# Blocks 11 and 12: q and k turned by DMA instead of by TensorE, and one x turned a unit sooner

## Chip, core and metric

One core of a Trainium2 chip runs the whole kernel. The metric is device time in microseconds; the time before is the median of three runs, 305.38 us (305.3 to 307.37). The profile comes from one further execution.

## What is computed

Attention in a sliding window with distance penalties, and behind it a layer norm and a two-layer MLP with a residual:

```python
scores = (q @ k.T) / sqrt(64) + slope[h] * -|i - j|     # only 0 <= i - j < 128
x = softmax(scores) @ v                                 # 8 batches, 8 heads, 576 tokens, 64 a head
x = x.transpose(0, 2, 1, 3).reshape(8, 576, 512)
xn = (x - mean) / sqrt(var + 1e-6) * g_ln
out = x + relu(xn @ w_ch1) @ w_ch2                      # 512 -> 2048 -> 512
```

Inputs and output are float32; the kernel loads them as float16 by casting DMAs and accumulates in float32.

## The kernel before

**Blocks and pairs.** The batches are taken two at a time (p = 0 to 3). The 576 tokens of such a pair of batches make nine blocks of 128 rows: blk 0 to 7 alternate between the two batches, and blk 8 holds the 64-token tails of both. Numbered through, there are 36 blocks; block n is (p, blk) = divmod(n, 9). q and k are loaded in pairs of blocks: (p, i) is the pair of blk 2i and 2i+1, so pair (1, 1) is blocks 11 and 12, (1, 2) is 13 and 14, (1, 3) is 15 and 16. The members of a pair are called its first and second half below.

**Turning q and k.** The scores need q and k with the 64 head elements on the partitions. There are two ways. With `turn` the pair is loaded in four DMAs (L256), TensorE makes 64 small transposes (L350, 32 for q and 32 for k) into two PSUM banks of the pool `ps_mm`, which has four, and VectorE and ScalarE copy one q and one k each out of them (L369, L370). With `turn_natural` the pair is loaded in six DMAs of another layout (q in four, L280; k in two, L277), and SyncE issues one transposing DMA for each half of q and of k (L383). The function `by_dma` decides: a pair goes by DMA if its number is at least `TURN_BY_DMA`, which is 13.

**The groups.** After attention, the blocks go through the MLP in groups: GROUPS = four of 2 blocks (groups 0 to 3), then seven of 4. A group has 16 units of the first layer (`mlp1`, L876 for the matmuls and L892 for the ScalarE relu, each unit filling one `ps_mm` bank) and a second layer (`mlp2`, L906), whose output a VectorE instruction (L1252) finishes and SyncE stores (L1272). The first layers of groups 0 and 1 run interleaved, as `mlp1_pair`.

**The order of the work** is written out by hand. TensorE, VectorE, ScalarE, SyncE and GpSimd run their instructions in the order of the program. `steps` is a list of attention steps; `weave_at(units, *places)` lays step after step behind the numbered units of a group, a place for each step. Before the loop stand the steps of blocks 0 to 9; from n = 8 the loop makes for each n four steps: values of block n (`values_at_once`, L598, with its x, L607), the turn of pair n + 3 where that is by TensorE, `centre` (xc, L639, with a transposing DMA of xc into xT on SyncE, L649), the scores of block n + 2 (`attend`, L502, exp on ScalarE, L513), the masks (L535) and the square of xc (L683). For pairs that go by DMA, q is issued with block m = n + 5 and k with m = n + 6 (`turn_natural` in `third`). Blocks 0 to 7, 10 and 11 have their x turned by TensorE (`turn_x`, L659); in groups 0 and 1 a VectorE or ScalarE instruction copies it out with the gain g (L666, L671).

**The queues.** GpSimd issues all loads in one order, AHEAD = 7 blocks ahead of the values; each of its DMAs waits on the one eight before it. Raw q and k tiles come from a pool of four for each tag (`raw_pool`); a load into a reused tile waits for the readers of that tile, TensorE's transposes or the transposing DMAs. SyncE issues the stores and the transposing DMAs of q, k and xc, in program order, each waiting on the SyncE DMA eight before. The turned tiles are pools of four (q) and five (k).

In the two lines of the loop that matter here, and in the place list of the interleaved first layers (L1308), the code before reads:

```python
if n + 3 < count and order[n + 3][1] % 2 == 0 and not by_dma(*order[n + 3]):
    step += turn_step(n + 3)          # n = 8: blocks 11 and 12
...
weave_at(mlp1_pair((0, 12), (0, 8), (12, NFB), (8, NFB)), 1, 2, 3, 3, 7, 7, 10, 18, 24, 28)
```

The seventh place, 10, belongs to the step x_step(3), the turn of block 3's x (L659 on TensorE, L666 on VectorE); unit 12 of that list is group 1's first, which reads it.

Of the kernel before, what the change touches and what calls it, by code (L numbers as in the profile page):

```python
# [39 lines left out]

SEVEN = 4

TURN_BY_DMA = 13

# [51 lines left out]
def kernel(  # L98
# [15 lines left out]
    NFB = FFN // P  # L114
# [5 lines left out]
    def pool(name, bufs, **kw):  # L120
        return ctx.enter_context(tc.tile_pool(name=name, bufs=bufs, **kw))
# [163 lines left out]
    def by_dma(p, blk):  # L285
        return p * NSLOT + blk >= TURN_BY_DMA

# [9 lines left out]
    order = [(p, blk) for p in range(NPAIR) for blk in range(NSLOT)]  # L297
# [393 lines left out]
    def inv_std(first, n):  # L691

        blocks = slice(first, first + n)
        rs = rstd[:, blocks]
        aa = small.tile([P, 4], FP32, tag="aa", name="aa")[:, 0:n]
        hh = small.tile([P, 4], FP32, tag="hh", name="hh")[:, 0:n]
        nc.vector.tensor_scalar(
            out=aa, in0=moments[:, blocks, 1], scalar1=EPS, scalar2=None, op0=ALU.add
        )
        nc.vector.tensor_scalar(  # L700
            out=hh.bitcast(I32),
            in0=aa.bitcast(I32),
            scalar1=1,
            scalar2=None,
            op0=ALU.logical_shift_right,
        )
        nc.vector.tensor_tensor(
            out=rs.bitcast(I32), in0=magic[:, 0:n], in1=hh.bitcast(I32), op=ALU.subtract
        )
        for _ in range(2):  # L710
            nc.vector.tensor_tensor(out=hh, in0=rs, in1=rs, op=ALU.mult)
            nc.vector.scalar_tensor_tensor(
                out=hh, in0=hh, scalar=-0.5, in1=aa, op0=ALU.mult, op1=ALU.mult
            )
            nc.vector.scalar_tensor_tensor(
                out=rs, in0=hh, scalar=1.5, in1=rs, op0=ALU.add, op1=ALU.mult
            )
# [11 lines left out]
    def turn_step(n, *how):  # L729
        p, blk = order[n]  # L730
        return [(turn, p, blk // 2) + how]

    def scores_step(n):
        return [(scores,) + order[n]]

    def values_steps(n):
        p, blk = order[n]
        ahead = place[min(n + AHEAD, count - 1)]
        return [
            [(load_until, ahead), (masks, p, blk), (values, p, blk, 0)],  # L740
            [(values, p, blk, 1), (centre, p, blk)],
        ]

    def x_step(n, copy=nc.vector.tensor_copy):
        return [(turn_x,) + home[n] + order[n] + (copy,)] if n < BY_DMA or n in IN_HASTE else []

    def variance_of(n):

        return [(variance, n)] + [(inv_std, n - 3, 4)] * (n % 4 == 3)

    def masks_of(n, *halves):
        return [(masks,) + order[n] + halves]

    def warm_step(n):
        return [[(warm, n)]]
# [3 lines left out]
    steps = warm_step(5) + [[(slopes,), (decay, m_full)]]  # L759
# [22 lines left out]
    steps += [[(decay, m_tail)] + x_step(5) + masks_of(6), scores_step(7) + variance_of(4), values_steps(6)[0]]  # L782

    steps += [values_steps(6)[1], x_step(6) + masks_of(7), *values_steps(7)]
    first_by_dma = order[TURN_BY_DMA][0], order[TURN_BY_DMA][1] // 2
    steps += [x_step(7) + variance_of(5) + variance_of(6) + [(turn_natural, "k") + first_by_dma]]
    steps += [turn_step(8) + variance_of(7), scores_step(8) + turn_step(9)]
    steps += [[(scores_tail, 0)] + scores_step(9) + masks_of(8) + masks_of(9)]


    for n in range(8, ONE_GO):
# [14 lines left out]
        for tag, m in (("q", n + 5), ("k", n + 6)):  # L806
            if m < count and order[m][1] % 2 == 0 and by_dma(*order[m]):
                p, blk = order[m]
# [9 lines left out]
    for n in range(ONE_GO, count):  # L818
# [12 lines left out]
        for tag, m in (("q", n + 5), ("k", n + 6)):  # L831
            if m < count and order[m][1] % 2 == 0:
                p, blk = order[m]
# [10 lines left out]
    def advance_to(n):  # L844
        nonlocal done
        while done < min(n, len(steps)):
            for f, *args in steps[done]:
                f(*args)
            done += 1
# [4 lines left out]
    def mlp1_pair(*spans):  # L854

        both = mlp1(0, (0, 1)), mlp1(1)
        last = [0, 0]
        for n, (first, end) in enumerate(spans):
            assert last[n % 2] == first
            last[n % 2] = end  # L860
            for _ in range(first, end):
                yield next(both[n % 2])
        for units in both:
            assert next(units, None) is None

    def mlp1(g, on_dve=()):
        xT = turned_x[g]
        w = w1 if g < FIRST_GROUPS else w1g
        cols = len(members[g]) * P

        at = g % 2 * cols if len(members[g]) == 2 else 0
        ht = hidden[g] = ht_all[:, :, at : at + cols]
        for fb in range(NFB):
            ps = ps_mm.tile([P, 4 * P], FP32, tag="mm", name="ps_m1")
            for kb in range(NKB):
                nc.tensor.matmul(  # L876
                    ps[:, 0:cols],
                    w[:, kb, fb * P : (fb + 1) * P],
                    xT[:, kb, 0:cols],
                    start=(kb == 0),  # L880
                    stop=(kb == NKB - 1),
                )
            if fb in on_dve:
                nc.vector.tensor_scalar(
                    out=ht[:, fb, :],
                    in0=ps[:, 0:cols],
                    scalar1=0.0,
                    scalar2=None,
                    op0=ALU.max,
                )  # L890
            else:
                nc.scalar.activation(  # L892
                    out=ht[:, fb, :], in_=ps[:, 0:cols], func=AF.Relu
                )
            yield cols
# [32 lines left out]
    def sum_w2(i):  # L928

        c = slice(4 * (i // 4), 4 * (i // 4) + 4)  # L930
        out, a, b = [(t1, b12, b11), (t3, b22, b12), (t2, b22, t1), (t4, b21, t2)][i % 4]
        minus(out[:, c], a[:, c], b[:, c])
# [343 lines left out]
    def weave_at(units, *places, seven=None, sums=None, more={}):  # L1276


        advance_to(done + places.count(-1))
        for u, _ in enumerate(units):  # L1280
            for f, *args in more.get(u, []):
                f(*args)
            if seven is not None:
                if u == 1:
                    inv_std(sum(GROUPS[:seven]), len(members[seven]))
                for i, c in SUMS_AT.get(u, []):
                    sum_hidden(seven, i, c)
            if sums is not None and u % 4 == 1:
                sum_w2(sums + u // 4)
            advance_to(done + places.count(u))  # L1290


    def start():
        nc.sync.dma_start(out=first_tables, in_=tables_dram[:, 0 : 3 * P])
        nc.sync.dma_start(out=g_sb, in_=moe_g_ln.rearrange("(kb p) -> p kb", p=P))
        load_until(place[7])
# [7 lines left out]
    with tc.manual_schedule(engines={engine.PE}):  # L1304
        with tc.manual_schedule(engines={engine.Activation, engine.DVE, engine.SP, engine.Pool}):
            start()
            advance_to(first)
            weave_at(mlp1_pair((0, 12), (0, 8), (12, NFB), (8, NFB)), 1, 2, 3, 3, 7, 7, 10, 18, 24, 28)  # L1308
            weave_at(mlp2(0, ((0, 8), (8, 12), (12, NFB))), 1, 4, 8, 10, 10, 12)
            weave_at(mlp2(1), 1, 3, 5, 7, 9, 13, 13)  # L1310
            weave_at(mlp1(2), 0, 4, 7, 9, 14)
            weave_at(mlp2(2), 1, 5, 9, 13, 13, 15, 15)

            weave_at(mlp1(3, (9, 10, 11)), 4, 7, 8, 10, 12, 15, sums=0)
            weave_at(mlp2(3), 0, 2, 3, 6, 9, 11, 12, sums=4)
            last = len(GROUPS) - 1
            for g in range(4, last):
                one, two = LEAD[g - 4]  # L1320
                early, late = ({u: [(sum_w1, i)] for u, i in at.items()} for at in W1_SUMS_AT.get(g, ({}, {})))
                if g == last - 1:
                    late[20] = [(sum_x, last, i) for i in (1, 2)]
                    late[24] = [(sum_x, last, i) for i in (3, 4)]
                    late[26] = [(inv_std, sum(GROUPS[:last]), len(members[last]))]
                late[4] = [(sum_hidden, g, 4, (0, half))]
                weave_at(mlp1(g, (6, 13)), *one, seven=g, more=early)
                weave_at(mlp2_seven(g), *two, more=late)
            units = mlp2_last(last)
            scores_psum.close()  # L1330
            ps_last = pool("ps_last", 1, space=PSUM)
            LAST_SUMS_AT = {
                u: [(sum_hidden, last, 3 + u % 2, (c, c + half // 2))]
                for u, c in ((2, 0), (4, half // 2), (3, 0), (5, half // 2))
            }
            mlp1_last(last, lambda: next(units), ps_last)
            weave_at(units, more=LAST_SUMS_AT)
# [31 lines left out]
```

## Time and profile before

| | |
|---|---|
| median of 3 runs | 305.38 us |
| the profiled execution | 304.42 us, of which its span 302.6 us |
| TensorE busy | 292.3 us (97%) |
| VectorE, ScalarE, GpSimd busy | 233.0, 184.9, 113.7 us |
| granted TensorE clock, mean | 0.998 |
| DMA, mean over the span | 126 GB/s |

Between the span and the time of the profiled execution lie 1.8 us. PE's busy time counts pipelined matmuls, so that a busy PE may still be slowed; the chain of waits tells which engine ends last at each point. SPq rows are what SyncE issues, POOL's DMA rows what GpSimd issues; a transfer's landing is given from its issue on.

### The profile page before, as it was taken

What the parts mean: (1) busy time and instruction counts of PE and PEld (TensorE: products, weight loads), DVE (VectorE), ACT (ScalarE), POOL (GpSimd) and SP (SyncE); (2) the same over time, 40 slices, a digit from 0 to 9 for tenths busy, and PEclk for the clock granted to TensorE, in tenths of its full rate; (3) what the DMA queues carried; (4) which work ended last, traced back from release to release, by engine and by line L of the source; (5) the groups of instructions that cost most, each with busy time, mean ns of one, the idle gap of its engine ahead of it and who ended that gap; (6) DMA issues with size and microseconds to landing.
All of it is one profiled execution on the core that took longest, in us unless ns stands there. A gap on an engine that the chain in (4) does not pass through costs nothing.

```text
span 302.6 us, 9271 instructions
## 1 busy us (share of the span) xinstructions
PE 292.3 (97%) x3783; PEld 201.0 (66%) x3783; DVE 233.0 (77%) x617; ACT 184.9 (61%) x338; POOL 113.7 (38%) x153
## 2 busy tenths in 40 slices
PE   7788999999999999999999999999999999999994
PEld 2367755866855578646865686568656865788883
DVE  3587778789996788668866886687798878878982
ACT  6577777868967883478357735674577456506500
POOL 8933768883773471594107170760000000000000
PEclk9999999999999999999999999999999999999999
DMA  9999999999999999999999999999571143006014
GB/s 93 167 197 204 192 170 165 196 149 102 143 132 177 164 157 116 156 206 140 95 156 136 128 104 172 168 132 101 122 126 27 38 101 74 20 17 141 3 35 104
DMA packets 150234, 38.03 MB, mean 126 GB/s; under 512 B 140688, under 2 KB 146080, under 8 KB 150192
## 3 DMA queue, kind: packets, MB, share of 16 engines
q0 software_dynamic: 103792, 18.46, 86.6%
q1 hardware_dynamic: 45840, 18.60, 38.7%
q8 instruction: 29, 0.48, 0.7%
q10 hardware_dynamic: 560, 0.39, 0.5%
q14 instruction: 13, 0.11, 0.1%
HBM read 36.90 MB, written 9.44 MB: 153 GB/s over the span
## 4 chain that ended last, share of the span: by engine, by line
PE 87%; DMA 4%; POOL 3%; DVE 2%; ACT 1%; issue 1%; DVEq 0%; POOLq 0%
PE ps_m L876 35%; PE ps_s L1106 22%; PE ps_m L906 9%; PE ps_sc L502 5%; PE ps_sc L598 4%; PE ps_q L1184 4%; DMA w<-in_moe_w_ch_dram 4%; PE ps_x L1000 3%; POOL vx L291 1%; POOL first L192 1%; DVE probs L535 1%; PE ps_pv L569 1%; PE ps_tr L350 1%; PE ps_t L1000 1%; PE ps_s L1000 1%
## 5 line engine op out<-in xcount | busy, mean ns | idle before, releaser
L876 PE MATMUL ps_m<-xT,w1g 128*128 128x512 f16 (+1 forms) x512 | 104.0, 353 | 0.1
L892 ACT ACTIVATE ht_all<-ps_m 128x512 f16<-128x512 f32 (+1 forms) x143 | 72.0, 511 | 38.3 <-PE ps_m L876 36.4
L876 PEld LDWEIGHTS <-w1g 128*128 128x128 f16 x512 | 47.7, 98 | 41.4 <-issue 0.3
L513 ACT ACTIVATE probs<-ps_sc 128x1024 f16<-128x1024 f32 x56 | 56.1, 1022 | 9.6 <-PE ps_sc L502 9.6
L291 POOL DMA_DIRECT2D vx<-in_v_dram x40 | 35.4, 893 | 67.8 <-PE ps_sc L598 59.7
L1106 PE MATMUL ps_s<-w,s 128*128 128x256 f16 x384 | 45.7, 273 | 0.0
L1106 PEld LDWEIGHTS <-s 128*128 128x128 f16 x384 | 36.8, 98 | 4.3 <-issue 0.2
L535 DVE TENSOR_TENSOR probs<-probs,m 128x1024 f16<-128x1024 f16 x56 | 36.3, 685 | 1.6 <-ACT probs L513 1.6
L1106 PE MATMUL ps_s<-w,ht_all 128*128 128x256 f16 x288 | 36.1, 273 | 0.0
L683 ACT ACTIVATE junk<-xc 128x512 f16<-128x512 f16 x28 | 17.7, 631 | 26.9 <-DVE xc L639 26.9
L906 PE MATMUL ps_m<-w,ht_all 128*128 128x512 f16 x128 | 31.5, 380 | 0.0
L1106 PEld LDWEIGHTS <-ht_all 128*128 128x128 f16 x288 | 27.4, 98 | 4.9
L926 DVE TENSOR_TENSOR s<-ht_all 128x1024 f16<-128x1024 f16 (+2 forms) x36 | 20.5, 571 | 11.9 <-ACT ht_all L892 10.9
L280 POOL DMA_DIRECT2D q<-in_q_dram x40 | 27.6, 707 | 4.2 <-PE ps_m L876 1.8
L502 PEld LDWEIGHTS <-k 64*64 64x64 f16 x1088 | 15.5, 107 | 13.5 <-issue 11.6
L607 DVE SCALAR_TENSOR_TENSOR x<-ps_sc,rec 128x512 f16<-128x512 f32 x32 | 22.1, 692 | 1.1
L1127 DVE SCALAR_TENSOR_TENSOR o<-ps_s,rstd,x 128x256 f32<-128x256 f32 x48 | 20.9, 478 | 2.6 <-PE ps_s L1106 2.2
L502 PE MATMUL ps_sc<-q,k 64*64 64x128 f16 (+1 forms) x1088 | 21.1, 211 | 1.2 <-ACT k L424 0.6
L277 POOL DMA_DIRECT2D k<-in_k_dram x20 | 17.9, 912 | 5.7 <-DMA k<-k 5.3
L606 DVE RECIPROCAL rec<-ps_sc 128x8 f32<-128x8 f32 x32 | 6.5, 204 | 16.3 <-PE ps_sc L598 16.2
L598 PEld LDWEIGHTS <-probs 128*128 128x128 f16 x384 | 15.9, 98 | 3.6
L906 PEld LDWEIGHTS <-ht_all 128*128 128x128 f16 x128 | 11.0, 98 | 10.6
(116 smaller groups left out, 374.6 us busy)
## 6 DMA issues: line engine op xcount, KB each, us to landing
out_dram<-o SPq DMA_DIRECT2D x64, 128.0 KB, 3.5
vx<-in_v_dram POOLq DMA_DIRECT2D x32, 128.0 KB, 6.8
w<-in_moe_w_ch_dram POOLq DMA_DIRECT2D x8, 512.0 KB, 11.3
k<-in_k_dram POOLq DMA_DIRECT2D x30, 128.0 KB, 7.2
q<-in_q_dram POOLq DMA_DIRECT2D x48, 64.0 KB, 5.6
q<-in_q_dram POOLq DMA_DIRECT2D x10, 128.0 KB, 5.3
out_dram<-o SPq DMA_DIRECT2D x9, 64.0 KB, 1.9
k<-in_k_dram POOLq DMA_DIRECT2D x8, 64.0 KB, 7.1
```

The costliest lines, as they stand in the source:

```text
L280: nc.gpsimd.dma_start(out=t[half, b], in_=tokens.rearrange("h (c r) d -> r c h d", r=2)[r],)
L291: nc.gpsimd.dma_start(out=vx[p0 : p0 + n, :, 0:D], in_=v[b, :, t0 : t0 + n, :].rearrange("h p d -> p h d"),)
L502: nc.tensor.matmul(in_halves(ps[cols, j, n, t, :])[:, r, queries], kt[rows, hp, cols], in_halves(qt[rows, b, hp])[:, r, queries], start=no ...
L513: nc.scalar.activation(out=dst.rearrange("p (n j) q -> p j n q", j=2), in_=ps.rearrange("p j n t q -> p j n (t q)"), func=AF.Exp, scale=in ...
L535: nc.vector.tensor_tensor(out=dst, in0=dst, in1=mask, op=ALU.mult)
L598: nc.tensor.matmul(ps[:, h, 0 : D + 1], pr[:, h, t, :], vext[(p * NSLOT + o) % NV][:, h, :], start=(n == 0), stop=(n == len(terms) - 1),)
L607: nc.vector.scalar_tensor_tensor(out=x.rearrange("p (h d) -> p h d", h=H), in0=ps[:, :, 0:D], scalar=1.0, in1=rec.unsqueeze(2).broadcast_t ...
L876: nc.tensor.matmul(ps[:, 0:cols], w[:, kb, fb * P : (fb + 1) * P], xT[:, kb, 0:cols], start=(kb == 0), stop=(kb == NKB - 1),)
L892: nc.scalar.activation(out=ht[:, fb, :], in_=ps[:, 0:cols], func=AF.Relu)
L906: nc.tensor.matmul(sums[at], ht[:, fb, at * P : (at + 1) * P], w2[:, fb, :], start=(fb == 0), stop=(fb == NFB - 1),)
L1106: nc.tensor.matmul(ps[:, pair, :], lhs[:, fb, at : at + P], rhs[:, fb, :], start=(first and pair == 0 and fb == 0), stop=(fb == half - 1), ...
L1127: nc.vector.scalar_tensor_tensor(out=outs[at][:, cols], in0=ps[:, pair], scalar=rstd[:, n : n + 1], in1=(xs[p, blk] if fresh else outs[at] ...
```

## The change

`TURN_BY_DMA` goes from 13 to 11, so that pair (1, 1), blocks 11 and 12, is loaded in the natural layout and turned by four transposing DMAs. They are issued, k before q, in the step that before issued the k of pair (1, 2): the step of x_step(7), behind unit 14 of the third group's first layer (`mlp1(2)`). The k of pair (1, 2) is issued at the end of the last step before the loop, that of the tail scores, of the scores of block 9 and of the masks of blocks 8 and 9. In the loop, the turn of pair (1, 1) by TensorE at n = 8 goes away. The place of x_step(3) goes from 10 to 9.

```diff
-TURN_BY_DMA = 13
+TURN_BY_DMA = 11
...
-    first_by_dma = order[TURN_BY_DMA][0], order[TURN_BY_DMA][1] // 2
-    steps += [x_step(7) + variance_of(5) + variance_of(6) + [(turn_natural, "k") + first_by_dma]]
+    (p, first_pair) = order[TURN_BY_DMA][0], order[TURN_BY_DMA][1] // 2
+    by_dma_first = [(turn_natural, tag, p, first_pair) for tag in "kq"]
+    steps += [x_step(7) + variance_of(5) + variance_of(6) + by_dma_first]
     steps += [turn_step(8) + variance_of(7), scores_step(8) + turn_step(9)]
     steps += [[(scores_tail, 0)] + scores_step(9) + masks_of(8) + masks_of(9)]
+    steps[-1].append((turn_natural, "k", p, first_pair + 1))
...
-            weave_at(mlp1_pair((0, 12), (0, 8), (12, NFB), (8, NFB)), 1, 2, 3, 3, 7, 7, 10, 18, 24, 28)
+            weave_at(mlp1_pair((0, 12), (0, 8), (12, NFB), (8, NFB)), 1, 2, 3, 3, 7, 7, 9, 18, 24, 28)
```

In the instruction streams, SyncE's order becomes: k of (1, 1) twice, q of (1, 1) twice, two stores, k of (1, 2) twice, the xc of block 8, two stores, q of (1, 2) twice. Before, the k of (1, 2) stood ahead of the first two stores, and nothing of (1, 1) was there. On GpSimd, the loads of pair (1, 1) are six in place of four, and the first load of q of pair (1, 3) waits for the two transposing DMAs of q of (1, 1) to be done, since it takes their raw tile; before, it waited for TensorE, and the k of (1, 3) waited for the transposing DMAs of k of (1, 2).

## The prediction

> **What bounds the kernel now.** I read the page first, then the chain of waits, then the timelines of SyncE's and GpSimd's queues round the place of the change.
>
> ```profile
> span 302.6 us, 9271 instructions
> ...
> PE 87%; DMA 4%; POOL 3%; DVE 2%; ACT 1%; issue 1%; DVEq 0%; POOLq 0%
> ```
>
> The chain runs through TensorE for 87% of the span, so an edit pays what it takes off TensorE's own stream, or off one of the few stretches where another engine ends last. The change touches two such stretches. The first is in the timeline near 25 us:
>
> ```profile
> 23.34 1.48 PE L876 MATMUL ps_m<-xT,w 128*128 128x256 f16 x12 [0.80 <-DMA w<-in_moe_w_ch_dram]
> 23.52 0.35 DVE L639 TENSOR_SCALAR xc<-x,mean 128x512 f16<-128x512 f16 x1
> ...
> 25.09 0.69 DVE L666 TENSOR_TENSOR xT<-ps_tx,g_sb 128x512 f16<-128x512 f16 x1 [1.22 <-PE ps_tx L659]
> ...
> 25.84 1.92 PE L876 MATMUL ps_m<-xT,w 128*128 128x256 f16 x16 [0.35 <-DVE xT L666]
> ```
>
> TensorE does three units, transposes block 3's x, does one more unit and then stands 0.35 us until VectorE has written xT. The second stretch is in the chain of waits (start, length, what), and, behind it, one TensorE row of the timeline. L513 is the exp of block 10's scores, L683 the square of block 8's xc, L892 the first relu:
>
> ```profile
> 71.75 0.73 PE ps_tr L350 x64
> ...
> 72.51 0.58 ACT q L369
> 73.09 0.64 ACT k L370
> 73.73 0.89 ACT own L513
> 74.62 0.61 ACT junk L683 x2
> 75.22 0.28 ACT ht_all L892
> ...
> 76.40 0.29 PE ps_sc L502 x8
> ...
> 78.41 2.30 PE ps_m L876 x20
> ...
> 85.03 0.49 PE ps_sc L598 x16
> 85.52 0.32 PE ps_sc L502 x8
> ...
> 97.25 0.52 PE ps_sc L502 x31
> ```
>
> ```profile
> 73.43 2.71 PE L876 MATMUL ps_m<-xT,w1g 128*128 128x256 f16 x20
> ```
>
> The 64 transposes of pair (1, 1) are on the chain with 0.73 us. Behind them the chain leaves TensorE: ScalarE's two copies push its exp, its square and then the first relu, and TensorE's fifth unit waits for a PSUM bank. The twenty matmuls from 73.43 take 2.71 us; the same twenty from 78.41, where nothing holds them, take 2.30. So 0.41 us are a stall that the turn causes. The rows at 76.40, 85.52 and 97.25 are the scores of blocks 11, 13 and 15: by then the turned q and k of their pairs must have landed.
>
> **The x a unit sooner.** The same matmuls run in another order: two units, the transposes, two units. Block 3's xc ends at 23.87; the second unit ends at about 23.34 + 8/12 of 1.48 = 24.33, so the transposes wait for nothing, VectorE starts half a microsecond sooner, and its 0.69 us end before the fourth unit does. The stall of 0.35 goes: bounds 0 (the weights of a later chunk hold TensorE instead; behind 25.84 no wait on a DMA stands in the chain before 72 us) and 0.35. I take 0.35.
>
> **The turn taken off TensorE.** Removed: 0.73 us of transposes, four copies, two PSUM banks. Between 0.73 (the stall stays) and 0.73 + 0.41 = 1.14 come off. Does the stall go? The first unit would start 0.73 sooner, at 72.70, and the fifth four units of 2.30/5 later, at 74.54. It needs the first relu. VectorE's side:
>
> ```profile
> 72.04 0.69 DVE L607 SCALAR_TENSOR_TENSOR x<-ps_sc,rec 128x512 f16<-128x512 f32 x1
> ...
> 73.78 0.36 DVE L639 TENSOR_SCALAR xc<-x,mean 128x512 f16<-128x512 f16 x1
> 74.06 0.74 DVE L1252 SCALAR_TENSOR_TENSOR o<-ps_m,rstd,x 128x512 f32<-128x512 f32 x1
> ```
>
> Between x (ends 72.73) and xc stand only the copies and a small mean, so xc8 ends near 73.3 in place of 74.14; ScalarE's exp is done by then, its square adds 0.61 and the relu 0.28: 74.2. That is in time by 0.3 us. I take 1.1. The full gain is then 0.35 + 1.1 = 1.45 us.
>
> [...]
>
> **What is added to the queues.** SyncE and GpSimd:
>
> ```profile
> 66.11 3.10 SPq L383 DMA_TRANSPOSE k<-k  x2
> 69.31 1.18 SPq L1272 DMA_DIRECT2D out_dram<-o  x2
> 74.30 1.20 SPq L649 DMA_TRANSPOSE xT<-xc  x1
> 75.59 1.20 SPq L1272 DMA_DIRECT2D out_dram<-o  x2
> 76.96 4.21 SPq L383 DMA_TRANSPOSE q<-q  x2
> ...
> 82.66 2.50 SPq L383 DMA_TRANSPOSE k<-k  x2
> 85.32 3.05 SPq L383 DMA_TRANSPOSE q<-q  x2
> ```
>
> ```profile
> 51.80 1.42 POOL L256 DMA_DIRECT2D q<-in_q_dram  x2
> 53.15 1.43 POOL L256 DMA_DIRECT2D k<-in_k_dram  x2
> ...
> 60.34 1.83 POOL L277 DMA_DIRECT2D k<-in_k_dram  x2 [0.20 <-PE ps_m L876]
> ...
> 65.16 2.74 POOL L280 DMA_DIRECT2D q<-in_q_dram  x4
> 73.16 1.77 POOL L277 DMA_DIRECT2D k<-in_k_dram  x2 [5.26 <-DMA k<-k]
> ```
>
> And the time from issue to landing (from the view of a tile, for a short window), in this order: k of (1, 1) loaded at 53.15; the two transposing DMAs from 66.11; that of q's first half at 76.96; that at 85.32.
>
> ```profile
> DMA to landing us min/median/max: 6.7/6.9/7.2
> DMA to landing us min/median/max: 5.1/5.4/5.6
> DMA to landing us min/median/max: 8.5/8.5/8.5
> DMA to landing us min/median/max: 8.8/8.8/8.8
> ```
>
> *Loads of (1, 1).* q takes 2.74 instead of 1.42, k 1.83 instead of 1.43: 1.7 us more on GpSimd. k goes from 54.5 to 56.4 and, 6.9 later, has landed by 61.4 and 62.4. The two loads more cover themselves: GpSimd waits later anyhow, 5.26 us ahead of 73.16.
>
> *k and q of (1, 1) on SyncE.* SyncE is free long before 66.11 (it stood waiting for the k of (1, 2)). k goes at 61.5, 2.5 to 3.1 us for two; q behind it, to 66.5 to 70.7 by its own issue times of 3.05 and 4.21. q's first half, issued at 64.0 to 64.6, lands 5.4 to 8.8 later, at 69.4 to 73.4. Block 11's scores come at 76.40 - 1.45 = 74.95. Cover of 1.5 us at least; the price with the cover gone is one for one.
>
> *The wait on GpSimd.* The loads of (1, 3) now start when q's second half of (1, 1) is done: issued about 66, landed at 71 to 75. Behind them are queued v, the tails' q and k, and all later loads. k of (1, 3) then starts 2.74 later, at 74 to 78 instead of 73.16, and its first half lands some 6.9 on, at 81 to 85. SyncE reaches that k only at 82.66, so at most 2.3 us show there. q of (1, 3) behind it landed at 85.32 + 8.8 = 94.1; block 15's scores run at 97.25, so with 0.85 us gained just 2.3 us of delay are covered.
>
> *q of (1, 2) is what is late next.* Before, its first half landed at 76.96 + 8.5 = 85.46, and block 13's scores run at 85.52: nothing to spare. With the gain, TensorE is there at 84.07. On SyncE, ahead of that q: the stores end at 70.1 (0.35 sooner), k of (1, 2) takes 2.5 to 3.1, to 72.7 to 73.3; the xc of block 8 is ready near 73.0 and takes 1.20, the stores 1.20, and with 0.1 between each, q starts at 75.6 to 76.0. Landing at 8.5: 84.1 to 84.5, late by 0 to 0.4. Its time to land is the open price. From below, 5.4; the nearest row is its own, 8.5; but it now has the k of (1, 2) close ahead in the queue, and beside it the loads of q of (1, 3), which before were issued at 65.16. These now fall into a lull, of which this is a row of the busy time by stretch (the last two numbers are the DMA share and GB/s):
>
> ```profile
> 72.00:74.00 2.00, 2.00 (x74) 1.38 (x63) 1.93 (x7) 1.49 (x3) 0.84 (x1) 1.00 0.19 62
> ```
>
> The lull takes part of what is added, so I put 0.4 on the 8.5: late by 0.4 to 0.8, middle 0.6. From above, 8.5 plus the two q issues at 4.21 that could stand in front again, 12.7: late by some 4.
>
> **Sum.** 0.35 + 1.1 - 0.6 = 0.85 us off the profiled 304.42, so 303.6. That execution was 0.96 under the median; the difference is carried over to the median: 305.38 - 0.85 = 304.5. Less than 1%, about what a measurement of this kernel can tell from no change, so the outcome would be within 1%.
>
> **Rivals.** *The full gain*: q of (1, 2) lands in time, since it starts a microsecond sooner and the lull absorbs the rest; 1.2 to 1.9 off, 304.0. Against it: 8.5 us of landing beside the same loads. [...]
>
> ```profile
> out_dram<-o SPq DMA_DIRECT2D x64, 128.0 KB, 3.5
> ...
> k<-k SPq DMA_TRANSPOSE x23, 5.9
> ```
>
> At a store's 3.5 us, q of (1, 2) would land at 79.5, far ahead of 84.07. *Slower*: the four added transfers lengthen the queue in which q of (1, 2) stands, and TensorE waits at block 13's scores. It decides from a landing of 85.5 on (no gain left); each microsecond later is one lost. With 10.5 to 12 us to land, or SyncE held by k of (1, 2), it is 86.5 to 88: 1 to 2.5 us slower, 306.9 in the middle; to 308.4 and over with 12.6 and more. *Block 11 itself waits*: k of (1, 1) lands only when the k of (1, 2) did before, at 66; then q's first half lands at 66.1 + 3.1 + 8.8 = 78, 3 us after its need, and all of SyncE's queue is behind it: 307 to 309. For it: two loads more ahead of it on GpSimd; against it: GpSimd's rows leave it 4 us.
>
> **Numbers.** Forecast 0.48 (304.2 to 305.1), full gain 0.20, slower by block 13 0.25, block 11 waits 0.07. The range takes the first two, to 303.3, and half of the third, to 307.0; what lies beyond is about 0.18. Over 1% slower (308.4) takes a third of the third case and half of the last: 0.12. Over 1% faster (302.3) is in no case as priced; I leave 0.04. Within: 0.84.
>
> **What would show it.** Right: no L350 rows near 72, the stall at 25.8 gone, twenty matmuls in 2.3 us, SyncE's k and q of (1, 1) from about 61.5, and TensorE waiting on a DMA of q at block 13's scores for under a microsecond. Wrong: a wait at blocks 11 or 15, k of (1, 1) issued at 64 or later, q of (1, 2) landing over 9.5 us or under 8.

## The result and the profile after

| | before | after |
|---|---|---|
| median, 22 runs each | 304.80 us (304.01 to 307.37) | 304.03 us (303.17 to 306.40) |
| ratio, 95% interval | | 0.9968 (0.9953 to 0.9983) |
| the profiled execution, its span | 304.42, 302.6 us | 303.43, 301.7 us |

The change gains a quarter to a third of one per cent (by the medians and by the ratio): less than 1%, but the interval stays below 1. With more runs of it the median before is 0.6 us lower than the one shown with the prediction. The page of the kernel after begins and goes on like this; the third line is a row of its queues (packets, MB, share of 16 engines), the last two are of its chain and of its groups:

```profile
span 301.7 us, 9149 instructions
...
PE 291.6 (97%) x3719; PEld 200.3 (66%) x3719; DVE 232.3 (77%) x615; ACT 184.0 (61%) x336; POOL 114.9 (38%) x155
...
q8 instruction: 29, 0.48, 0.7%
...
PE 88%; DMA 5%; DVE 2%; issue 1%; POOL 1%; ACT 0%; DVEq 0%; POOLq 0%
...
L280 POOL DMA_DIRECT2D q<-in_q_dram x44 | 30.2, 700 | 13.7 <-DMA q<-q 7.2
```

TensorE carries the chain as before. GpSimd's 7.2 us of waiting for a transposing DMA of q is the new wait that the forecast described. The first stretch, in the timeline after:

```profile
23.08 1.05 PE L878 MATMUL ps_m<-xT,w 128*128 128x256 f16 x8 [0.53 <-DMA w<-in_moe_w_ch_dram]
...
24.19 4.07 PE L878 MATMUL ps_m<-xT,w 128*128 128x256 f16 x35
...
24.39 0.69 DVE L666 TENSOR_TENSOR xT<-ps_tx,g_sb 128x512 f16<-128x512 f16 x1 [0.54 <-PE ps_tx L659]
```

Two units, the transposes, and then TensorE runs on without a wait: VectorE's xT ends inside the next matmuls, and the idle 0.35 us ahead of 25.84 are gone. The second stretch, in the chain of waits after (start, length, what):

```profile
70.21 0.85 PE ps_sc L598 x24
71.06 0.15 PE ps_sc L502
71.21 0.34 issue
71.55 0.36 PE ps_sc L502 x9
71.91 0.97 PE ps_m L908 x4
72.88 2.18 PE ps_m L878 x20
75.06 0.26 PE ps_sc L598 x8
75.32 0.29 PE ps_sc L502 x8
...
83.95 0.49 PE ps_sc L598 x16
84.44 0.29 PE ps_sc L502 x8
```

The transposes and the detour through ScalarE are gone, and TensorE stays on the chain through block 13's scores at 84.44. But inside block 10's scores, after the third of sixteen matmuls, stands a line that no step of the forecast has: 0.34 us of "issue", time in which TensorE waited for nothing that the profile shows. And the queues, SyncE's rows first:

```profile
61.55 2.69 SPq L383 DMA_TRANSPOSE k<-k  x2
64.42 2.65 SPq L383 DMA_TRANSPOSE q<-q  x2
...
76.39 2.56 SPq L383 DMA_TRANSPOSE q<-q  x2
...
74.55 2.72 POOL L280 DMA_DIRECT2D q<-in_q_dram  x4 [7.23 <-DMA q<-q]
```

From the view of the tile q, for the issues at 64.42 and at 76.39:

```profile
DMA to landing us min/median/max: 8.1/8.1/8.1
```

```profile
DMA to landing us min/median/max: 5.9/5.9/5.9
```

Block 11's q is there at 72.5, 2.8 us ahead of its scores at 75.32. The first half of q of (1, 2) is there at 82.3, 2.1 us ahead of 84.44.

**Where the 0.9 us of span came from**, by the chains of the two executions: 0.26 at 23 us, because a load of weights ended sooner (23.08 for 23.34; both kernels read it alike, and in the traces below with the full warm-up and no small matmuls the unit starts between 22.77 and 23.49, so this is taken as chance); 0.43 between there and the values of block 8 (70.90 before, 70.21 after), the x step; 0.39 between those values and block 11's scores (76.40 before, 75.32 after), the turn. Of these 1.08 us, 0.40 are lost again at 143 us, in the timeline after:

```profile
143.35 1.77 POOL L277 DMA_DIRECT2D k<-in_k_dram  x2 [0.22 <-issue]
...
143.56 0.77 DVE L639 TENSOR_SCALAR xc<-x,mean 128x512 f16<-128x512 f16 x1
```

and in that of before:

```profile
144.68 0.35 DVE L639 TENSOR_SCALAR xc<-x,mean 128x512 f16<-128x512 f16 x1
```

VectorE is on the chain there, and its xc took 0.77 instead of 0.35 us while GpSimd issued a load. In the traces of seven kernels below, the change's second among them, this xc took 0.35, so it is an accident of that execution, not of the change. The remaining 0.2 us of gain arise behind it and were not traced.

### The profile page after: what moved, and what is told of

It is laid out like the page before. It is cut to its first block, busy times and chain, and to the rows that moved or that the text cites. A ratio compares the mean times of both kernels' runs of the same rounds, so it can differ in the third digit from the quotient of the medians.

```text
span 301.7 us, 9149 instructions
## 1 busy us (share of the span) xinstructions
PE 291.6 (97%) x3719; PEld 200.3 (66%) x3719; DVE 232.3 (77%) x615; ACT 184.0 (61%) x336; POOL 114.9 (38%) x155
## 4 chain that ended last, share of the span: by engine, by line
PE 88%; DMA 5%; DVE 2%; issue 1%; POOL 1%; ACT 0%; DVEq 0%; POOLq 0%
PE ps_m L878 36%; PE ps_s L1108 22%; PE ps_m L908 10%; PE ps_sc L502 5%; PE ps_sc L598 4%; PE ps_q L1186 4%; DMA w<-in_moe_w_ch_dram 4%; PE ps_x L1002 3%; DMA first<-in_k_dram 2%; DVE probs L535 1%; POOL first L192 1%; PE ps_pv L569 1%; PE ps_t L1002 1%; PE ps_s L1002 1%; PE ps_tx L659 1%
## 5 line engine op out<-in xcount | busy, mean ns | idle before, releaser
L280 POOL DMA_DIRECT2D q<-in_q_dram x44 | 30.2, 700 | 13.7 <-DMA q<-q 7.2
L908 PE MATMUL ps_m<-w,ht_all 128*128 128x512 f16 x128 | 31.5, 380 | 0.0
L502 PEld LDWEIGHTS <-k 64*64 64x64 f16 x1088 | 15.6, 107 | 14.0 <-issue 12.1
L502 PE MATMUL ps_sc<-q,k 64*64 64x128 f16 (+1 forms) x1088 | 21.3, 212 | 1.5 <-ACT k L424 0.7
L277 POOL DMA_DIRECT2D k<-in_k_dram x22 | 19.7, 910 | 3.4 <-DMA k<-in_k_dram 2.1
L908 PEld LDWEIGHTS <-ht_all 128*128 128x128 f16 x128 | 11.0, 98 | 10.6
```

Source lines behind the costliest of these rows:

```text
L280: nc.gpsimd.dma_start(out=t[half, b], in_=tokens.rearrange("h (c r) d -> r c h d", r=2)[r],)
L502: nc.tensor.matmul(in_halves(ps[cols, j, n, t, :])[:, r, queries], kt[rows, hp, cols], in_halves(qt[rows, b, hp])[:, r, queries], start=no ...
L908: nc.tensor.matmul(sums[at], ht[:, fb, at * P : (at + 1) * P], w2[:, fb, :], start=(fb == 0), stop=(fb == NFB - 1),)
```

## The experiments

Two questions: do the two parts add up, and what is the gap in block 10's scores? Edits are given against the kernel after unless said otherwise. A time is a median of its runs; a ratio is that to the kernel before, from runs on the same chip.

**The change once more, and its two parts alone.** No edit; then, from the change, the place back to 10:

```diff
-            weave_at(mlp1_pair((0, 12), (0, 8), (12, NFB), (8, NFB)), 1, 2, 3, 3, 7, 7, 9, 18, 24, 28)
+            weave_at(mlp1_pair((0, 12), (0, 8), (12, NFB), (8, NFB)), 1, 2, 3, 3, 7, 7, 10, 18, 24, 28)
```

and the kernel before with the place 9 alone.

> The changed kernel, unchanged, to see which rows of its profile come back. In its first profile TensorE stands 0.34 us inside block 10's scores, with no wait that the profile shows, and this eats most of what the transposes took. Theory A (the supply of TensorE's instructions at that place, a property of this instruction stream): the gap comes back within 0.1 us of 0.34 at the same scores. Rival B (chance of one execution): no gap over 0.1 us there, and block 11's scores then come 0.3 us sooner after block 8's values (3.9 instead of 4.26 us). Also: block 18's xc or another one near 143 us takes 0.77 instead of 0.35 us because GpSimd issues a load beside it (theory C, it comes back, since GpSimd's queue is late by the change) or not (chance). Time: 0.995 to 0.998 of the kernel before.

> The change without the move of block 3's x: the place stays 10. My theory: the sum splits, about 0.4 to 0.6 us come from the turn (0.73 of transposes and 0.41 of stall off, 0.3 to 0.5 given back in a gap in block 10's scores), ratio 0.998 to 0.9985; the stall of 0.35 us near 25 us stays. Rival: all of the gain is the turn's, ratio 0.9965 to 0.997.

> The kernel before with only the place of block 3's x moved from 10 to 9. My theory: the stall of 0.35 us at the first unit of the second group goes and nothing takes its place: 0.35 to 0.45 us off, ratio 0.9985 to 0.999, and block 11's scores come 0.35 to 0.45 us sooner after the weights' landing. Rival: the time is set further on by ScalarE's copies or by DMA, and the ratio is 1.000 within its interval.

Measured: the change again 303.88 us, ratio 0.9982 (0.9959 to 1.0005); the turn alone 304.74, 0.9998 (0.9984 to 1.0012); the x step alone 304.28, 0.9988 (0.9969 to 1.0007). By time alone neither part can be told from nothing, nor can the whole change in this repeat, whose interval reaches 1; the traces tell more. The repeat answers the question that was asked of it: the gap comes back, but not within 0.1 us of 0.34. With the x step alone the stall at 25 us is gone, and what eats the gain is the q of (1, 2), in the chain of that kernel:

```profile
75.98 9.94 DMA q<-q
...
85.96 0.36 PE ps_sc L502 x8
```

SyncE issued it a microsecond sooner than in the kernel before, yet it took 9.9 instead of 8.5 us to land, and TensorE stood at block 13's scores. That is the late q that the forecast feared, but in the layout of before. In the turn alone the gap in block 10's scores is 1.11 us, and in the change's second trace, of an execution of 307.19 us, it is 2.19:

```profile
71.83 0.15 PE ps_sc L502
71.98 2.19 issue
74.17 0.53 PE ps_sc L502 x8
...
76.52 2.69 PE ps_m L878 x20
```

The same place each time, between the same two matmuls, with a length that varies. It is in no trace of a kernel in which TensorE turns blocks 11 and 12.

**What the gap is.** In part 3 of the page the queue q8 has 29 "instruction" transfers of 0.48 MB in all, and part 1 counts 3719 matmuls and as many weight loads: 7438 instructions. Divided by the 29, that is some 16 KB and 256 instructions to a transfer; that each brings TensorE's next 256 is an estimate from these counts. The number of transfers moves with the length of TensorE's program: the kernel below with one pair more by DMA has 7310 such instructions and 28 transfers, the one with 111 small matmuls 7660 and 30. One such read can be found in the DMA view for two microseconds (40 slices of 0.05 us), as the one slice far above the others. For the windows 67 to 69 us of before, the same of after, and 70 to 72 us of the change's second trace:

```profile
GB/s 146 161 146 128 138 120 123 126 126 120 120 458 131 128 103 110 105 121 120 133 126 136 138 138 138 146 156 166 156 166 159 161 164 166 154 136 149 141 123 118
...
q8 instruction: 1, 0.02, 4.2%
```

```profile
GB/s 182 189 166 146 136 156 144 151 159 164 159 159 146 161 151 156 129 164 136 154 149 156 154 161 141 161 146 161 159 164 146 154 143 451 141 143 151 146 138 154
...
q8 instruction: 1, 0.02, 4.1%
```

```profile
GB/s 161 156 159 159 166 156 154 164 166 151 161 164 159 148 166 156 161 161 177 159 177 172 492 141 174 192 157 146 151 146 136 129 149 146 143 136 125 100 69 20
...
q8 instruction: 1, 0.02, 3.6%
```

The twelfth slice is 67.6, the 34th is 68.7, the 23rd of the last is 71.1. In every trace that has the gap near block 10, here and below, it ends some 2.5 to 3.2 us after the read. So the reading is: TensorE ran out of instructions, because the read of its next 256 came late among the other transfers. In the kernel before, the same border of 256 falls three matmuls into the 64 transposes, since these stand just ahead of block 10's scores; there the read at 67.6 came in time. To test the reading, the program was shifted against the borders of 256. One kernel runs 35 small matmuls of ones more (`small_ones`; 70 instructions with their weight loads) at the start, another 111 (222 instructions), and a third leaves out all but the last four of the matmuls that warm TensorE up. The text recorded for the third counts 17 of 21; the pages count 3719 matmuls in the change and 3704 in it, so 15 of 19 are gone, 30 instructions:

```diff
+    steps += [[(small_ones, 35)]]
     steps += [[(turn_first, 1)], *warm_step(2), scores_step(1)]
```

```diff
-    steps = warm_step(5) + [[(slopes,), (decay, m_full)]]
+    steps = warm_step(0) + [[(slopes,), (decay, m_full)]]
```

(and likewise at the other warm-up steps but the last).

> The change with 35 small matmuls of ones more near 8 us, where TensorE waits for a load: they compute nothing and only move every later TensorE instruction 70 places back in its stream. Theory F (the gap in block 10's scores is TensorE waiting for its next 256 instructions, which are read over the DMA engines in pieces of 16 KB, and come late because the transposing DMAs and loads are in the way): the gap does not stay at block 10's scores, it moves 70 instructions forward in the program, to the first second-layer matmul behind block 9's scores (L908 of the change), and is longer, 1.5 to 4 us, since TensorE works through the 256 instructions before it in some 3.2 us instead of 5.5; the time is 0.5 to 2 us longer than the change's. Rival W (block 10's scores wait for something of their own, such as the turned tiles or the score bank): the gap stays in block 10's scores.

> The same with 111 small matmuls, 222 places: the border of 256 instructions that fell into block 10's scores falls 34 instructions further on, into the first layer's units behind them, and TensorE takes 6.6 us for the 256 before it instead of 5.5. Theory F: the gap at block 10's scores is gone; at the border, after 8 or so matmuls of the first layer, a gap of 0 to 1 us is left; the time is 0.3 to 1 us under the change's, ratio to the kernel before 0.993 to 0.9955. Rival W: the gap stays in block 10's scores, and the time is the change's or longer by what the small matmuls cost.

> The change without 17 of its 21 warming matmuls (all but the last four, near 14 us), which compute nothing: every later TensorE instruction stands 34 places sooner in its stream, so that the border of 256 instructions falls behind block 10's scores instead of into them, and TensorE takes some 6.6 us for the 256 instructions before it instead of 5.5. Theory F (late instructions): no gap in block 10's scores; at most 1.2 us at the last second-layer matmuls behind them; if the start does not suffer (TensorE waits for weights until 23 us), 0.3 to 1 us faster than the change, ratio to the kernel before 0.993 to 0.996. Rival W (block 10's scores wait for something of their own): the gap stays in block 10's scores. Rival S (the slower start costs more): no gap, but the first unit after 23 us comes later and the time is that of the change or longer.

Measured: 306.73 us, 1.0063 (1.0033 to 1.0092); 307.78, 1.0091 (1.0062 to 1.012); 305.58, 1.0017 (0.9993 to 1.004). The chain of the kernel with 70 instructions more (its L919 is L908, its L512 is L502), and then that of the kernel with 30 fewer:

```profile
67.99 0.47 PE ps_sc L512 x28
68.45 1.65 issue
70.10 1.89 PE ps_m L919 x8
```

```profile
74.24 0.54 PE ps_m L908 x2
74.78 0.36 issue
75.14 0.60 PE ps_m L908 x2
```

With 70 more, the gap stands earlier in the work: ahead of the eight second-layer matmuls that come before block 8's values. Those eight, the 24 of the values and three of the scores lie between there and the old place: 35 matmuls, as many as were added. With 30 fewer, it stands later: in the middle of the four second-layer matmuls behind block 10's scores, 13 scores and two of the four on, 15 matmuls for 15 removed. Nothing is left in block 10's scores in either. A wait for data would have stayed with its matmul. With 222 more, no gap is left near block 10, and one of 2.61 us is at the start, behind the added matmuls, in the chain of that kernel (its profile is of an execution of 311.33 us, against a median of 307.78, so only the order of events is read from it):

```profile
8.07 1.03 PE ps_warm L346 x111
...
10.70 2.61 issue
```

So the place moved as was forecast. The times did not follow: by the ratios the three are 2.9, 3.7 and 1.5 us slower than the change, where 0.5 to 2 us slower was forecast for the first and 0.3 to 1 us faster for the others. In the trace with 35 matmuls more these cost nothing by the next weights (the unit that waits for them starts at 23.15, 23.08 in the change), but the gap is longer. In the one with 15 fewer the start is slower: the first eight matmuls of the first layer, at 18.31, take 1.82 us (1.05 at 16.61 in the change), and block 10's scores start 2.8 us later. Where the 3.7 us of the third come from isn't shown.

**What delays the read.** Candidates: the four transposing DMAs that were added, the loads of GpSimd that run beside them, or GpSimd's new order. Five kernels. One gives raw q a fifth tile, so that GpSimd doesn't wait for the transposing DMAs:

```diff
-    raw_pool = pool("raw", 4)
+    raw_pool = {"q": pool("raw_q", 5), "k": pool("raw_k", 4)}
```

(and `raw_pool[tag]` where tiles are taken from it). One moves the loads of (1, 1) ahead of those of v of blocks 9 and 10 in GpSimd's list, so that the transposing DMAs go sooner, and one does so with the shorter warm-up:

```diff
+    moved = [l for l in loads if l[0] == load_natural and l[3:] == (1, 1)]
+    at = loads.index((load_v, 1, 0))
+    rest = [l for l in loads if l not in moved]
...
+    loads = rest[:at] + moved + rest[at:]
```

One has no transposing DMAs of blocks 11 and 12 (VectorE sets their turned q and k to zero instead), with all else in place; one has no loads of v of blocks 13 and 14:

```diff
+        if (p, i) == (1, 1):
+            nc.vector.memset(t, 0.0)
+            return
```

```diff
+        if p * NSLOT + blk in (13, 14):
+            return
```

> The change with five raw tiles for q in place of four, so that the load of q of blocks 15 and 16 need not wait for the transposing DMAs of q of blocks 11 and 12. GpSimd's wait of 7.2 us ahead of that load goes, and its loads from there on start 2 to 5 us sooner. Theory (the late queue of GpSimd costs what is lost later, the 0.4 us near 143 us): about 0.4 us faster than the change, ratio to the kernel before 0.995 to 0.996. Rival 1 (GpSimd's lateness is covered everywhere): the same time as the change. Rival 2 (q of blocks 13 and 14 then lands later, beside more loads, as in the kernel before): TensorE waits at block 13's scores, and the time is 0.3 to 1 us longer than the change's.

> The change with the loads of q and k of blocks 11 and 12 issued on GpSimd ahead of the v of blocks 9 and 10, not behind them. Their transposing DMAs can start up to 1.8 us sooner, near 59.7 instead of 61.5, and are issued before TensorE asks for its next 256 instructions near 65.6. TensorE's instruction stream is the same. Theory F with the transposing DMAs as what is in the way: the read of those instructions comes 0.5 to 1.5 us sooner (67.2 to 68.2 instead of 68.7 to 71.1 us), the gap at block 10's scores is 0 to 0.5 us, and the time 0.3 to 1 us under the change's. Rival (the loads of GpSimd are what is in the way, or both): the read stays at 68.7 or later, the gap at 0.3 to 2.2 us, and the time is the change's.

> Both edits. Theory F: no gap over 0.3 us between 68 and 76 us; 0.5 to 1.2 us faster than the change, ratio to the kernel before 0.992 to 0.9955. Rival: as for each of the two, the larger time.

> The change without its four transposing DMAs of blocks 11 and 12: their turned q and k are set to zero on VectorE, so those two blocks attend wrongly; the loads, and every TensorE instruction, stay. Which transfers keep TensorE's next 256 instructions waiting? Theory X (the transposing DMAs in flight): the read near 68.7 to 71.1 us comes at 67.7 or sooner, as in the kernel before, no gap over 0.2 us in block 10's scores, and the time is 0.3 to 1.5 us under the change's, ratio to the kernel before 0.991 to 0.996. Theory Y (the loads of GpSimd): the read stays at 68.7 or later and the gap at 0.3 to 2.2 us.

> The change without the loads of v of blocks 13 and 14, which GpSimd issues at 65.0 and 66.4 us (those two and later blocks use an older v in their place). Theory X (the transposing DMAs are what keeps TensorE's instructions waiting): the read stays at 68.7 or later, and the gap in block 10's scores at 0.3 to 2.2 us. Theory Y (the loads are): the read comes at 67.7 or sooner and no gap over 0.2 us is left.

Measured: the fifth tile 305.74 us, 1.004 (1.002 to 1.006); the loads sooner 304.6, 1.0005 (0.9983 to 1.0026), with the shorter warm-up 305.5, 1.0033 (1.0013 to 1.0053); without the transposing DMAs 306.07, 1.0045 (1.0019 to 1.0072); without those loads of v 303.33, 0.9961 (0.9944 to 0.9979). Wherever a gain was forecast, none came: by the ratios, the fifth tile, the loads sooner and the kernel without the transposing DMAs are 1.1 to 2.3 us slower than the change, and the one without the loads of v takes the same. The loads sooner with the shorter warm-up, forecast to have no gap over 0.3 us, have one of 1.09 us in the place that the shorter warm-up alone gave it. The times alone mislead here, so the reads were looked up in the traces, and set against a fixed point of the work, the start of the eight second-layer matmuls (L906 or L908) at 66 to 67 us (from the chain; in the third row from the timeline):

| kernel | start of the eight | read | behind it | gap in block 10's scores |
|---|---|---|---|---|
| before | 66.77 | 67.6 | 0.8 | none |
| x step alone | 65.80 | 66.7 | 0.9 | none |
| no transposing DMAs of 11 and 12 | 67.08 | 67.8 | 0.7 | none |
| no loads of v of 13 and 14 | 66.72 | 69.0 | 2.3 | 0.06 |
| the change | 66.08 | 68.7 | 2.6 | 0.34 |
| the turn alone | 66.57 | 70.0 | 3.4 | 1.11 |
| fifth raw q tile | 66.69 | 70.4 | 3.7 | 1.83 |
| loads of (1, 1) sooner | 66.57 | 70.4 | 3.8 | 1.16 |
| the change, second trace | 66.89 | 71.1 | 4.2 | 2.19 |

Without the transposing DMAs of blocks 11 and 12 the read comes 0.7 to 0.9 us behind that point, in three kernels; with them 2.3 to 4.2, in six. The third row is the cleanest: it has the loads of the change and lacks only those four DMAs, and its chain at block 10 is

```profile
72.11 0.85 PE ps_sc L601 x22
72.96 0.34 PE ps_sc L505 x12
73.30 0.97 PE ps_m L911 x4
```

with no gap in the scores (L505). So it is the added transposing DMAs that push the read back; one trace of that kernel shows it, and the other eight agree. That kernel is slow for other reasons: its two memsets of 0.48 us stand in VectorE's queue ahead of the statistics that TensorE's next work waits for, and TensorE stands 2.08 us at block 13's scores, whose q took 9.8 us to land; GpSimd had its loads of (1, 3) behind it by then (from 66.89, in place of 74.55) and was issuing those that follow. The loads of v are not needed for a late read: without them it still comes 2.3 us behind the point. But the gap is 0.06, where 0.34 to 2.19 stand with them, and the chain of that kernel is the best that was seen:

```profile
71.59 0.15 PE ps_sc L504
71.74 0.06 issue
71.79 0.36 PE ps_sc L504 x9
```

Whether 0.06 is due to the missing loads or is the short end of the spread isn't settled by one trace. Sending the transposing DMAs sooner didn't help (k of (1, 1) at 58.30 and q at 62.41 in place of 61.55 and 64.42; read at 70.4), so which of them holds the read, and by what, stays open. And taking away the wait of GpSimd, which the forecast counted as a cost, gains nothing: without it the kernel is slower, by a ratio whose interval doesn't meet that of the change on the same chip. Why that is, whether through a later read or through the loads that then run beside the transposing DMAs, is not shown.

**One pair more by DMA.** `TURN_BY_DMA` at 9: blocks 9 and 10 are turned by DMA as well; their k and q are issued ahead of those of blocks 11 and 12, in the same step, and their turn by TensorE goes away.

```diff
-TURN_BY_DMA = 11
+TURN_BY_DMA = 9
...
-    steps += [x_step(7) + variance_of(5) + variance_of(6) + by_dma_first]
-    steps += [turn_step(8) + variance_of(7), scores_step(8) + turn_step(9)]
+    second = [(turn_natural, tag, p, first_pair + 1) for tag in "kq"]
+    steps += [x_step(7) + variance_of(5) + variance_of(6) + by_dma_first + second]
+    steps += [turn_step(8) + variance_of(7), scores_step(8)]
...
```

> The change taken one pair further: blocks 9 and 10 are turned by DMA too, their k and q issued ahead of those of blocks 11 and 12 in the same step, and their 64 transposes and four copies are gone. Theory F: with 128 instructions fewer the border falls 128 instructions further on and the 256 before take some 7 us, so no gap over 0.5 us is left near 71 us; 0.58 us of transposes more come off; but block 9's scores, near 67 us, need the k and q issued after 61 us, with 5 to 8 us to land and four behind them: TensorE may wait there for 1 to 3 us. 0.5 us faster to 2 us slower than the change. Rival (no wait at block 9, the queue is quick enough): 1 to 1.5 us faster than the change, ratio to the kernel before 0.991 to 0.994.

Measured: 311.84 us, 1.0206 (1.0168 to 1.0244). In its chain two waits:

```profile
59.15 17.79 DMA q<-q x2
...
82.06 9.83 DMA q<-q
```

The first ends at block 11's scores, the second at block 13's; TensorE stands 1.92 us and 5.76 us there, and only 0.74 us at block 10's, so the waits come later and are longer than was forecast, and by the ratios the kernel is some 7 us slower than the change, not 2 at most. With four transposing DMAs more in SyncE's queue, the cover that the forecast worked out for block 11 (1.5 us at least) is gone, and all q behind it come late too.

## Why the prediction was right, and where it wasn't

The time, the sign and the size came out: 0.85 us were forecast, 0.77 measured between the medians. That the size came out so closely is luck: the sum has the same total by different terms, one of them wrong and one that nobody had seen.

- **The x a unit sooner, 0.35.** Right: the stall is gone, and 0.43 us arrive at block 8's values (47.1 us behind the start of the first unit on the new weights, for 47.6 before; the x step alone has 47.1 too). In the change's second trace it is lost again on the way (47.5), with 0.25 us of "issue" at 42.1.
- **The turn off TensorE, 1.1.** The mechanism was right, the size too large. The transposes were priced by their length in the chain, 0.73. By the starts of TensorE's rows in the timeline of before, the scores begin 0.53 us behind them (71.68 to 72.21), and behind values instead of transposes the scores themselves take 0.15 more (0.50 for 0.35, with the gap taken off). That leaves 0.38. The stall of 0.41 went, as worked out from VectorE's and ScalarE's rows; by the same starts it gave 0.37 (2.53 in place of 2.90 us from the twenty matmuls to the next scores). The 0.41 had set a length of the timeline, 2.71, against one of the chain, 2.30; the timeline's own row at 78.35 has 2.36, which leaves 0.35. Together 0.75 of the 1.1.
- **q of (1, 2) late, -0.6.** This step failed. It landed 5.9 us after its issue, not 8.9, and TensorE did not wait, as the rival of the full gain had it; the forecast itself had named a landing under 8 as a sign of being wrong. The loads of q of (1, 3), for which it added 0.4, did run beside it (GpSimd's row at 74.55, this q at 76.39). But they stand behind GpSimd's long wait, and with that wait this q landed in 5.9 to 7.9 us in seven of the eight traces that have a landing for it (9.5 in the one of 311.33 us). In the four kernels whose loads of (1, 3) had no such wait behind the transposing DMAs of q of (1, 1) (before, the x step alone, the fifth tile, no transposing DMAs of 11 and 12) it took 8.1 to 9.9; with one pair more by DMA, 9.8. So the wait that was counted as a risk goes with a quicker q; that it is the cause is not shown. That TensorE's wait was on the edge is confirmed by the x step alone, where q took 9.9. In the change this q did not land at a store's pace either, which would have had it there at 79.5: it came at 82.3. Its 5.9 us and the 8.1 of block 11's stand between the medians of 3.4 for a store of 128 KB and of 8.0 to 8.6 for GpSimd's loads of that size on this page.
- **What stood in its place** was no rival at all: the gap, -0.34 in this trace and up to 2.19 in others. 0.38 + 0.37 - 0.34 = 0.41, and 0.39 were measured. And the 0.40 lost at 143 us and the 0.26 of sooner weights are accidents that the forecast could not hold. The forecast asked of the four added transfers whose queue they stand in and whose data they delay; it did not ask what else goes over the DMA engines. TensorE's program does.
- **Block 11** doesn't wait, its q was there 2.8 us ahead, and the queue did as forecast: k of (1, 1) at 61.55 (61.5 forecast), GpSimd's q of (1, 3) at 74.55, its k at 77.2 (74 to 78).

Open is how large the gap is in the median execution; the traces have 0.34 and 2.19, at 303.43 and 307.19 us, on both sides of it.

## What to carry to other kernels

Where an engine stands still for nothing that the trace shows, look at whether the place moves with the program when instructions are added or taken away ahead of it; here it did (35 matmuls sooner for 35 added, 15 later for 15 removed), and I read it as the program's own delivery. Then look for the read in the DMA view, and compare it with a kernel without the suspected transfers: here taking them away brought the read forward, and sending them sooner did not. A DMA that replaces work of a saturated engine can cost that engine time in this way too (0.34 and 2.19 us in the two traces of this change), not only by its own landing time. And price work that is taken off a pipelined engine by the starts of its neighbours, not by its own length (0.38 us for a length of 0.73 here).

## What was not expected of the hardware

**The clock after a gap.** Rows of the busy time by stretch, for the change's second trace and for the fifth raw tile (the third number from the right is TensorE's granted clock):

```profile
74.00:76.00 2.00, 1.83 (x17) 0.84 (x18) 0.00 (x0) 1.24 (x2) 1.24 (x2) 0.51 1.23 295
76.00:78.00 2.00, 2.00 (x13) 1.36 (x12) 1.44 (x3) 0.83 (x4) 2.00 (x4) 0.64 1.35 71
```

```profile
74.00:76.00 2.00, 2.00 (x10) 1.19 (x9) 0.96 (x2) 1.72 (x4) 1.79 (x3) 0.66 2.09 156
76.00:78.00 2.00, 2.00 (x12) 1.39 (x11) 0.99 (x2) 1.05 (x3) 2.00 (x4) 0.50 2.95 129
```

Behind gaps of 2.19 and 1.83 us the clock fell to a half (means of 0.51 and 0.64, and of 0.66 and 0.50, over two stretches of two microseconds each), and the twenty matmuls took 2.69 and 3.74 us instead of 2.18. Behind gaps of 1.65 us (35 small matmuls), 1.16, 1.11, 1.09 and 0.34 it stayed at 1.00 in the same view. But the length alone does not decide it: in the kernel without the transposing DMAs TensorE kept its pace behind a longer wait, the one ahead of this row (in the chain, the six and ten second-layer matmuls behind it took 1.41 and 2.27 us, as in the change), and so it did behind the 1.92 us at block 11's scores with blocks 9 and 10 by DMA (the next twelve and twenty of the first layer took 1.43 and 2.30, as in the kernel before).

```profile
87.92 0.37 PE L505 MATMUL ps_sc<-q,k 64*64 64x128 f16 x16 [2.08 <-DMA q<-q]
```

So a long gap can cost more than its length: in the change's second trace the gap is 1.85 us longer than in the first, the scores and the four matmuls behind it take 1.0 more (0.53 and 1.82 for 0.36 and 0.97) and the twenty 0.5 more, 3.4 of the 4.15 us by which block 11's scores come later in it (79.47 for 75.32); the span of 305.4 is 3.7 longer. Why the clock fell behind 1.83 and 2.19, while the pace held behind 1.92 and 2.08, is not shown.

**VectorE beside GpSimd.** The same xc of 128x512 took 0.35 us alone and 0.77 beside a load that GpSimd was issuing, on the chain at 143 us: an accident of timing that is worth as much as either part of the change. It is not the only one. Of the 54 rows of xc in the timelines of both kernels between 11 and 199 us, the 14 with no load being issued beside them took 0.35 or 0.36; of the 40 beside one, 15 took 0.45 to 0.77 and the others 0.35 to 0.39. What sets the 15 apart is not shown.
